# A three-stage kernel whose list scheduler gets other durations, with a smaller DMA scratch, a second row buffer and two more weight slots

## The chip, the cores and the metric

One core of a Trainium2 chip runs the whole program. The metric is the device time of one launch in microseconds (us); lower is better. The core's engines work in parallel and wait for each other by semaphores: PE (TensorE: matmuls; PEld is its weight load), DVE (VectorE), ACT (ScalarE), POOL (GpSimd) and SP (SyncE, which here only issues DMAs, in a fixed order). Each engine works through its own list of instructions in order, so an instruction that waits holds up everything behind it on that engine.

## The reference

Three stages, one feeding the next. B = 4, H = 8, S = 576, D = 64, so 2304 tokens of 512 numbers.

```python
scores = scale * np.matmul(q, k.transpose(0, 1, 3, 2))
ret = scores * Dmat[None, :, :, :]            # decay by distance, causal
x = np.matmul(ret, v)                         # -> 2304 x 512
gate = 1.0 / (1.0 + np.exp(-(x @ w_gate)))    # 512 -> 1536
x = gate * (x @ w_val) @ w_out                # 1536 -> 512
noisy = x @ w_gate2 + np.log1p(np.exp(x @ w_noise)) * noise
top2 = np.argpartition(-noisy, 2, axis=1)[:, :2]     # 2 of 8 experts
out[mask] += w[mask, k, None] * (np.maximum(x[mask] @ w1[e], 0.0) @ w2[e])   # 512 -> 1024 -> 512
```

The weights of the second stage (here called moe1) come as 64-bit floats, all else as 32-bit floats.

## The kernel before, in words

**Arithmetic.** Every large matmul is made as three passes over a value split in two parts (high part and remainder), so each weight and each activation is first split: a cast writes the high part, a subtraction the remainder. 

**Stages.** *Attention* goes by units of two heads: transposes of k and q (PE, L469) that ACT copies out as K (L473), for the later chunk of a sequence a product QF on DVE (L479), scores on PE (L518), the product P of scores and decays on DVE (L525), then av on PE (L535 to L543). *moe1* goes by blocks of 256 tokens and 128-wide slices of the 1536: gv on PE (`up`, L1007), a sigmoid on ACT (L605), sig on DVE (L607), gh on ACT and DVE (L609, L610), then acc on PE (L616). Its first third (half 0, four slices) runs between attention's units, and the partial sums go through a buffer `row` (ACT copy L629 in `part_out`) to DRAM. Half 1 does the other eight slices; `x2_out` (L633 and on) loads the partial sum (L637), adds it (L639), splits the row by 16-bit halves (a copy, in a helper at L283), stores it as x2d (L646), turns it by a DMA transpose on SP (`turn`, L947), joins the halves again (x2T, L283) and makes the routing logits on PE (L668, L671). *Routing* (`route`) takes five groups of token tiles, ranks them (rk, L819), and scatters two table entries per token tile with indirect DMAs of POOL (T, L857). *moe2* loads the tables (L870, L876), gathers an expert's rows on POOL (xr, L913), turns them (xq, L947; for the first two parts xtp on PE, L943), splits them into gxT (L962), then `up` (L1007), hT on ACT and DVE (L1012, L1014), `down` y (L1020), the weighting yo (L1025, L1027) and POOL's scatters of it (L1036). From the second expert on POOL also fetches the rows written before (ag, L1000). Each expert has two parts (s = 0, 1 for the first expert, s = 2, 3 for the second and so on).

**Weights.** `weight64` converts a 64-bit float slice: a DMA r64 (L307), two ACT passes (L308, L310), on DVE the triple L315, L316, L317, an integer add on POOL (L319), a cast on ACT (L320) and a subtraction on DVE (L321). There are 36 such conversions. `weight32` loads raw (L328, three buffers), casts it (L283, on ACT or DVE) and subtracts (L331, on DVE or POOL). Finished weights lie in slots of one ring, "w": NSLOT_A from the start and NSLOT_B more once attention's buffers are given up (`open2`).

**The order.** No engine's list is written by hand. Each operation is declared with an engine (or a choice of engines), a duration from a formula (`t_act`, `t_dve`, `t_fast`, `t_pool`, `t_pe`), a priority, the buffers that it reads and writes, and for a DMA an amount `nbytes` for the shared DMA time line and a `tail` until the data are there. `Order.run` then simulates: at each step it takes, over all engines, the operation that can start first, and among those within .02 us of that on an engine the one of the best priority; LAT is added when an operation waits for another engine. A ring that is full makes the next writer wait. The resulting order is what the engines get. The main lines are:

```python
c.append((s, o.prio, o.seq, o))
t0 = min(x[0] for x in c)
s, p, q, o = min((x for x in c if x[0] <= t0 + .02), key=lambda x: (x[1], x[2]))
dma = max(dma, s + us + 0.6) + o.nbytes
o.end = dma
o.end += o.tail
```

Of the kernel before, what the change touches and what calls it, by code (L numbers as in the profile page):

```python
# [65 lines left out]
P_UNIT, P_CONV, P_MOE1, P_MOE2 = 4.0, 6.0, 1000.0, 2000.0  # L66
P_CONV_OFF2, P_CONV2, LEAD_W, LEAD_A = 80.0, 6.0, 8, 8
P_CONV_OFF, P_X, P_EV, P_ROUTE, P_FILL = 7.0, -700.0, -900.0, -900.0, 900.0
ROWB = 1
DMA_TAIL = 1.0  # L70
P_HALF, TURNED, X2T, X2H, X2P, X2R, XF = 0.0, 14, 1, 1, 2, 1, 1

TURN_FROM = 2
# [11 lines left out]


def t_act(n):
    return .05 + .0009 * n


def t_dve(n):
    return .06 + .00105 * n


def t_fast(n):
    return .06 + .00053 * n


def t_pool(n):
# [20 lines left out]
class Order:  # L120


    LAT = 0.17

    def __init__(self):
        self.ops, self.rings, self.live, self.chain, self.bufs = [], {}, {}, {}, {}
# [138 lines left out]
                    put(d)  # L265


NSLOT_A, NSLOT_B = 18, 6


class Kern:
# [20 lines left out]
    def weight64(self, src, shape, prio):  # L292

        nc, op = self.nc, self.op
        n = 512
        raw = self.buf("r64", lambda _: self.cv.tile([128] + shape[:-1] + [2 * shape[-1]], I32, name="r64", bufs=NCV[0]))
        t1 = self.buf("t1", lambda _: self.cv.tile([128, n], I32, name="t1", bufs=NCV[1]))
        t2 = self.buf("t2", lambda _: self.cv.tile([128, n], I32, name="t2", bufs=NCV[2]))
        w = self.wbuf(shape, "w")
        pat = "p k (f t) -> p (k f) t" if len(shape) == 2 else "p (f t) -> p f t"  # L300

        def word(i):
            return raw.ap.rearrange(pat, t=2)[:, :, i]

        def wv(i):
            return (w.ap.rearrange("p a k f -> p a (k f)") if len(shape) == 2 else w.ap)[:, i]
        op("SP", .5, lambda: nc.sync.dma_start(raw.ap, src), w=[raw], prio=prio - LEAD_W, nbytes=1.45, tail=DMA_TAIL)  # L307
        op("ACT", t_act(n), lambda: nc.scalar.activation(f(t1.ap), f(word(1)), AF.Abs), r=[raw], w=[t1], prio=prio)  # L308

        op("ACT", t_act(n), lambda: nc.scalar.activation(t2.ap, word(0).bitcast(U32), AF.Copy, scale=2.0 ** -29),  # L310
           r=[raw], w=[t2], prio=prio)


        def high():
            nc.vector.tensor_scalar(f(t1.ap), f(t1.ap), E_MIN, E_MAX, op0=ALU.max, op1=ALU.min)  # L315
            nc.vector.tensor_scalar(t1.ap, t1.ap, 3, 0x3fffffff, op0=ALU.logical_shift_left, op1=ALU.bitwise_and)  # L316
            nc.vector.scalar_tensor_tensor(t1.ap, word(1), -0x40000000, t1.ap, op0=ALU.bitwise_and, op1=ALU.bitwise_or)  # L317
        op("DVE", .27 + 2 * t_fast(n) + t_dve(n), high, r=[raw, t1], w=[t1], prio=prio)
        op("POOL", t_pool(n), lambda: nc.gpsimd.tensor_add(t2.ap, t1.ap, t2.ap), r=[t1, t2], w=[t2], prio=prio)  # L319
        op("ACT", t_act(n), lambda: nc.scalar.copy(wv(0), f(t1.ap)), r=[t1], w=[w], prio=prio)  # L320
        op("DVE", t_dve(n), lambda: nc.vector.tensor_sub(wv(1), f(t2.ap), f(wv(0))), r=[t2, w], w=[w], prio=prio)  # L321
        return w

# [309 lines left out]
    def x2_out(self, t, acc, prio):  # L633
        nc, op = self.nc, self.op
        part = self.buf("part", lambda _: self.rt.tile([128, DM], F32, name="part", bufs=X2P))
        row = self.buf("x2", lambda _: self.rt.tile([128, DM], F32, name="x2", bufs=X2R))
        op("SP", .5, lambda: nc.sync.dma_start(part.ap, self.p2d[t * 128:(t + 1) * 128, :]), r=[self.p2[t]], w=[part],  # L637
           prio=prio, nbytes=.73, tail=DMA_TAIL)
        op("DVE", t_dve(DM), lambda: nc.vector.tensor_add(row.ap, acc.ap, part.ap), r=[acc, part], w=[row], prio=prio)  # L639
        self.x2[t] = self.buf(None, None)  # L640

        xh = self.buf("x2h", lambda _: self.rt.tile([128, DM], I32, name="x2h", bufs=X2H))
        op(None, {"ACT": t_act(2 * DM), "DVE": t_fast(2 * DM), "POOL": t_pool(3 * DM)},
           lambda e: self.split(e, xh.ap, row.ap),
           r=[row], w=[xh], prio=prio + P_HALF)
        op("SP", .5, lambda: nc.sync.dma_start(self.x2d[t * 128:(t + 1) * 128, :], xh.ap), r=[xh], w=[self.x2[t]],  # L646
           prio=prio + P_HALF, nbytes=.73, tail=DMA_TAIL)
        xT = self.buf("x2T", lambda _: self.rt.tile([128, KD, 128], F32, name="x2T", bufs=X2T))
        if t < TURNED:
            xq = self.buf("x2q", lambda _: self.rt.tile([128, 2 * KD, 128], U16, name="x2q", bufs=1))  # L650
            op("SP", .5, lambda: self.turn(xq.ap, xh.ap), r=[xh], w=[xq], prio=prio + P_HALF, nbytes=.9, tail=DMA_TAIL)
            for w in range(2):
                op(None, {"ACT": t_act(DM), "DVE": t_fast(DM)}, lambda e, w=w: self.join(e, xT.ap, xq.ap, w), r=[xq], w=[xT], prio=prio + P_HALF)
        else:
            tp = self.buf("x2p", lambda _: self.ps_rt.tile([128, KD, 128], F32, name="x2p", tag="x2p"))

            def transposes():
                for k in range(KD):
                    nc.tensor.transpose(tp.ap[:, k], row.ap[:, k * 128:(k + 1) * 128], self.ident)
            op("PE", .45, transposes, r=[row], w=[tp], prio=prio)  # L660
            op(None, {"ACT": t_act(DM), "DVE": t_dve(DM)}, lambda e: self.copy(e, xT.ap, tp.ap), r=[tp], w=[xT], prio=prio)

        lg = self.buf("lg", lambda _: self.ps_lg.tile([128, 2, 128], F32, name="lg", tag="lg"))
        lT = self.buf("lT", lambda _: self.lT)

        def logits():
            for k in range(KD):
                nc.tensor.matmul(lg.ap[32 * k:32 * k + 32, 0], self.wgn[:, k], xT.ap[:, k], start=True, stop=True)  # L668
        op("PE", .27, logits, r=[xT, self.rset], w=[lg], prio=prio)
        op("ACT", t_act(128), lambda: nc.scalar.copy(lT.ap, lg.ap[:, 0]), r=[lg], w=[lT], prio=prio)  # L670
        op("PE", .11, lambda: nc.tensor.transpose(lg.ap[:, 1], lT.ap, self.ident), r=[lT], w=[lg], prio=prio)  # L671
        self.lgb[t] = self.buf(None, None)
        op("DVE", .25, lambda: nc.vector.tensor_reduce(
            self.lgs[:, t], lg.ap[:, 1].rearrange("p (g e) -> p e g", e=32)[:, :2 * E], axis=mybir.AxisListType.X, op=ALU.add),
            r=[lg], w=[self.lgb[t]], prio=prio)
        for g in GROUPS:
            if t == g[-1]:
                self.route(g, prio)
# [285 lines left out]
    def gather(self, s):  # L964

        op = self.op
# [6 lines left out]
        for t in range(nt):  # L973
# [9 lines left out]
                op("PE", .45, lambda x=x, xf=xf: self.columns(x.ap, xf.ap), r=[xf], w=[x], prio=p)  # L983
            else:
                xq, x = self.buf("xq", self.xq_tile), xf
                op("SP", .5, lambda xq=xq, xr=xr: self.turn(xq.ap, xr.ap), r=[xr], w=[xq], prio=p, nbytes=.9, tail=DMA_TAIL)
                for w in range(2):
                    op(None, {"ACT": t_act(DM), "DVE": t_fast(DM)}, lambda e, xq=xq, xf=xf, w=w: self.join(e, xf.ap, xq.ap, w),
                       r=[xq], w=[xf], prio=p)
# [310 lines left out]
```

## Time and profile before

| | |
|---|---|
| runs | 1124.95 us median of 3 (1123.38 to 1125.94) |
| the profiled execution | 1132.48 us, span 1130.8 us, mean granted TensorE clock 0.982 of full speed |
| busy share of the span | PE 94%, PEld 83%, DVE 52%, ACT 33%, POOL 25% |
| largest groups on PE | gv 339.0 us, up 236.4, y 221.5, acc 178.8 |
| DMA | 120.14 MB, mean 106 GB/s |

A time line row gives the start of a run of like instructions, its length, engine, line, what is written from what, how many, and in brackets how long the engine had stood idle before, and for whom. Rows with "q" (SPq) are DMA issues in the engine's queue; their length is the time that the queue was held, waiting included. A busy share is an average over stages; stages are looked at apart by a table of stretches.

### The profile page before, as it was taken

The numbers are of one execution on the slowest core, as the hardware profiler recorded it, in microseconds if no ns is written. First come the engines' busy times: TensorE is split into PE (matmuls) and PEld (weight loads), VectorE is DVE, ScalarE is ACT, GpSimd is POOL, SyncE is SP. The second block draws the span as 40 slices with busy tenths as digits, with TensorE's granted clock in tenths as the row PEclk, the third lists the DMA queues.
The fourth block names the chain that finished last, engine by engine and source line by source line (L and its number), as shares of the span: only waits on it lengthen the run. The fifth ranks groups of instructions, "written<-read, shape, count | busy, mean of one in ns | idle before, by whom it ended". The sixth has DMA issues, their size and how long they took to land. (4 is left out here: it accounts for less than half of the span.)

```text
span 1130.8 us, 18154 instructions
## 1 busy us (share of the span) xinstructions
PE 1066.9 (94%) x6965; PEld 937.3 (83%) x6966; DVE 591.9 (52%) x1360; ACT 368.5 (33%) x783; POOL 284.5 (25%) x288
## 2 busy tenths in 40 slices
PE   9779997999999999999998898799999999999996
PEld 6546776999889898889988787789888989898985
DVE  4998447322942425332556866546464747474421
ACT  5666325323732322222224323223222323232110
POOL 2322002000310001300205424444434343433230
PEclk9999998999999999999999999899999999999998
DMA  7898316101400511331123427836464756564210
GB/s 183 206 235 204 85 43 173 57 20 38 149 20 1 112 25 33 58 57 25 33 57 122 122 67 183 203 97 187 108 172 123 182 131 187 130 189 92 75 53 14
DMA packets 193564, 120.14 MB, mean 106 GB/s; under 512 B 124286, under 2 KB 169854, under 8 KB 193472
## 3 DMA queue, kind: packets, MB, share of 16 engines
q1 hardware_dynamic: 180480, 94.17, 33.5%
q0 software_dynamic: 12992, 24.75, 7.5%
q8 instruction: 56, 0.92, 0.4%
q14 instruction: 36, 0.29, 0.1%
HBM read 91.23 MB, written 28.94 MB: 106 GB/s over the span
## 5 line engine op out<-in xcount | busy, mean ns | idle before, releaser
L1007 PEld LDWEIGHTS gv<-xs,w 128*128 128x128 f32 x2592 | 329.9, 192 | 15.3 <-DVE sig L607 3.5
L1007 PE MATMUL gv<-xs,w 128*128 128x256 f32 x2592 | 339.0, 285 | 2.9 <-DVE sig L607 2.9
L1007 PE MATMUL up<-gxT,w 128*128 128x256 f32 (+1 forms) x1536 | 236.4, 314 | 9.8 <-DVE hT L1014 9.6
L1007 PEld LDWEIGHTS up<-gxT,w 128*128 128x128 f32 x1536 | 231.4, 192 | 13.8 <-DVE hT L1014 11.6
L1020 PE MATMUL y<-w,hT 128*128 128x512 f32 (+1 forms) x960 | 221.5, 390 | 0.0
L1020 PEld LDWEIGHTS y<-w,hT 128*128 128x128 f32 x960 | 178.0, 188 | 38.1
L616 PE MATMUL acc<-w,gh 128*128 128x512 f32 x648 | 178.8, 406 | 9.1 <-ACT row L629 4.9
L616 PEld LDWEIGHTS acc<-w,gh 128*128 128x128 f32 x648 | 113.7, 192 | 34.4 <-DVE gh L610 5.8
L607 DVE TENSOR_TENSOR sig<-sig,gv 128x256 f32<-128x256 f32 x108 | 45.3, 419 | 170.5 <-ACT sig L605 170.2
L1012 ACT ACTIVATE hT<-up 128x256 fp32r<-128x256 f32 (+1 forms) x128 | 56.2, 439 | 239.2 <-PE up L1007 129.6
L605 ACT ACTIVATE sig<-gv 128x256 f32<-128x256 f32 x108 | 41.5, 384 | 217.8 <-PE gv L1007 213.8
L857 POOL DMA_INDIRECT T<-ent,di x36 | 36.5, 1014 | 272.0 <-DVE ent L853 262.7
L319 POOL TENSOR_TENSOR t<-t,t 128x512 int32<-128x512 int32 x36 | 50.3, 1398 | 188.6 <-ACT t L310 108.1
L1027 DVE SCALAR_TENSOR_TENSOR yo<-y,tab,ag 128x512 f32<-128x512 f32 (+1 forms) x35 | 26.0, 743 | 118.7 <-PE y L1020 118.7
L1014 DVE SCALAR_TENSOR_TENSOR hT<-up,hT 128x256 fp32r<-128x256 f32 (+1 forms) x128 | 62.5, 488 | 47.7 <-ACT hT L1012 47.6
L331 DVE TENSOR_TENSOR w<-raw,w 128x512 fp32r<-128x512 f32 x117 | 79.9, 688 | 7.8 <-ACT w L283 6.6
L913 POOL DMA_INDIRECT xr<-x2d,tab x40 | 42.9, 1073 | 162.2 <-DMA xq<-xr 149.6
L610 DVE TENSOR_TENSOR gh<-sig,gh 128x256 fp32r<-128x256 f32 x108 | 46.3, 428 | 27.3 <-ACT gh L609 27.1
L609 ACT CAST gh<-sig 128x256 fp32r<-128x256 f32 x108 | 43.9, 407 | 46.9 <-DVE sig L607 46.7
L1036 POOL DMA_INDIRECT p2d<-yo,tab x38 | 39.6, 1042 | 56.9 <-DVE yo L1027 44.3
L1036 POOL DMA_INDIRECT out_dram<-yo,tab x35 | 38.4, 1097 | 43.9 <-DVE yo L1027 34.4
L283 ACT CAST w<-raw 128x512 fp32r<-128x512 f32 x53 | 32.7, 619 | 47.2 <-PE y L1020 23.8
(180 smaller groups left out, 947.4 us busy)
## 6 DMA issues: line engine op xcount, KB each, us to landing
raw<-in_moe_w_dram SPq DMA_DIRECT2D x128, 256.0 KB, 3.2
r<-in_moe_w_gate_dram SPq DMA_DIRECT2D x12, 512.0 KB, 4.6
r<-in_moe_w_val_dram SPq DMA_DIRECT2D x12, 512.0 KB, 4.6
r<-in_moe_w_out_dram SPq DMA_DIRECT2D x12, 512.0 KB, 4.4
p2d<-row SPq DMA_DIRECT2D x18, 256.0 KB, 2.0
part<-p2d SPq DMA_DIRECT2D x18, 256.0 KB, 3.7
x2d<-x2h SPq DMA_DIRECT2D x18, 256.0 KB, 3.4
kn<-in_k_dram SPq DMA_DIRECT2D x24, 128.0 KB, 3.7
```

What stands on the lines that cost most here:

```text
L319: op("POOL", t_pool(n), lambda: nc.gpsimd.tensor_add(t2.ap, t1.ap, t2.ap), r=[t1, t2], w=[t2], prio=prio)
L331: lambda e: self.eng(e).tensor_sub(w.ap[:, 1], raw.ap, f(w.ap[:, 0])), r=[raw, w], w=[w], prio=prio)
L607: op("DVE", t_dve(BLK), lambda sig=sig, gv=gv: nc.vector.tensor_mul(sig.ap, sig.ap, gv.ap[:, 1, :]), r=[gv, sig], w=[sig], prio=p)
L609: op("ACT", t_act(BLK), lambda sig=sig, gh=gh: nc.scalar.copy(gh.ap[:, 0, :], sig.ap), r=[sig], w=[gh], prio=p)
L610: op("DVE", t_dve(BLK), lambda sig=sig, gh=gh: nc.vector.tensor_sub(gh.ap[:, 1, :], sig.ap, f(gh.ap[:, 0, :])), r=[sig, gh], w=[gh], prio=p)
L616: nc.tensor.matmul(a[tt].ap, gh.ap[:, p, tt * 128:tt * 128 + 128], wo.ap[:, q, :], start=first and n == 0, stop=last and n == 2)
L913: self.nc.gpsimd.indirect_dma_start(out=xr, out_offset=None, in_=self.x2d[0:n, :], in_offset=bass.IndirectOffsetOnAxis(ap=idx, axis=0), bo ...
L1007: self.nc.tensor.matmul(ps[:, :n], w1[:, p, k, :], xT[:, q, k, :n], start=k == 0 and j == 0, stop=k == KD - 1 and j == 2)
L1012: self.nc.scalar.activation(hT[:, ft, 0, :n], ps[:, :n], AF.Relu)
L1014: self.nc.vector.scalar_tensor_tensor(hT[:, ft, 1, :n], ps[:, :n], 0.0, f(hT[:, ft, 0, :n]), op0=ALU.max, op1=ALU.subtract)
L1020: self.nc.tensor.matmul(y, hT[:, ft, p, t * 128:t * 128 + 128], w2[ft][:, q, c], start=ft == 0 and j == 0, stop=ft == NF2 - 1 and j == 2)
L1036: return self.nc.gpsimd.indirect_dma_start(out=dst[:, :], out_offset=bass.IndirectOffsetOnAxis(ap=idx, axis=0), in_=yo, in_offset=None, bo ...
```

## The change

It alters constants of the planner, the sizes of three resources, and the declared costs of three kinds of DMA:

- `t_act`, `t_dve`, `t_fast` (duration of an ACT or DVE instruction of n elements a partition) and LAT are larger;
- DMA_TAIL goes from 1.0 to 1.4; the r64 load counts 1.6 of DMA time instead of 1.45, with .6 more tail; a turn (both uses of L947) counts 1.25 us on SP instead of .5, less DMA time, and .3 less tail than DMA_TAIL;
- the ring `row` gets a second buffer, the weight slots go from 18 + 6 to 19 + 7;
- the program is built with 4,096 bytes of scratch for POOL's DMAs in place of the default of 16,384.

```diff
-ROWB = 1
-DMA_TAIL = 1.0
+ROWB = 2
+DMA_TAIL = 1.4
...
 def t_act(n):
-    return .05 + .0009 * n
+    return .13 + .0009 * n
 def t_dve(n):
-    return .06 + .00105 * n
+    return .08 + .00112 * n
 def t_fast(n):
-    return .06 + .00053 * n
+    return .1 + .0006 * n
...
-    LAT = 0.17
+    LAT = 0.22
...
-NSLOT_A, NSLOT_B = 18, 6
+NSLOT_A, NSLOT_B = 19, 7
...
-        op("SP", .5, lambda: nc.sync.dma_start(raw.ap, src), w=[raw], prio=prio - LEAD_W, nbytes=1.45, tail=DMA_TAIL)
+        op("SP", .5, lambda: nc.sync.dma_start(raw.ap, src), w=[raw], prio=prio - LEAD_W, nbytes=1.6, tail=DMA_TAIL + .6)
...
-            op("SP", .5, lambda: self.turn(xq.ap, xh.ap), r=[xh], w=[xq], prio=prio + P_HALF, nbytes=.9, tail=DMA_TAIL)
+            op("SP", 1.25, lambda: self.turn(xq.ap, xh.ap), r=[xh], w=[xq], prio=prio + P_HALF, nbytes=.7, tail=DMA_TAIL - .3)
...
-                op("SP", .5, lambda xq=xq, xr=xr: self.turn(xq.ap, xr.ap), r=[xr], w=[xq], prio=p, nbytes=.9, tail=DMA_TAIL)
+                op("SP", 1.25, lambda xq=xq, xr=xr: self.turn(xq.ap, xr.ap), r=[xr], w=[xq], prio=p, nbytes=.7, tail=DMA_TAIL - .3)
...
-    nc = bacc.Bacc("TRN2", target_bir_lowering=False, num_devices=1)
+    nc = bacc.Bacc("TRN2", target_bir_lowering=False, num_devices=1, dynamic_dma_scratch_size=4096)
```

The order moves on every engine. Three places follow; numbers behind names are the program's buffer numbers and differ between the two orders.

First pair: DVE in attention, from the QF product of one unit to the first P product of the next (L315 to L317 and L321 are weight conversions). Before:

```order
L479 TENSOR_TENSOR QF_882<-K_821,gq_113 128x320
L436 TENSOR_TENSOR ks_890<-kn_836,gk_110 128x512
L321 TENSOR_TENSOR w_853<-t2_803,w_853 128x512
L315 TENSOR_SCALAR t1_784<-t1_784 128x512
L316 TENSOR_SCALAR t1_784<-t1_784 128x512
L317 SCALAR_TENSOR_TENSOR t1_784<-r64_704,t1_784 128x512
L315 TENSOR_SCALAR t1_916<-t1_916 128x512
L316 TENSOR_SCALAR t1_916<-t1_916 128x512
L317 SCALAR_TENSOR_TENSOR t1_916<-r64_867,t1_916 128x512
L479 TENSOR_TENSOR QF_953<-K_888,gq_113 128x320
L321 TENSOR_TENSOR w_935<-t2_911,w_935 128x512
L525 TENSOR_TENSOR P_968<-sc_948,gd_112 128x2x320
```

With the change, the same place:

```order
L479 TENSOR_TENSOR QF_866<-K_758,gq_113 128x320
L321 TENSOR_TENSOR w_830<-t2_763,w_830 128x512
L436 TENSOR_TENSOR ks_888<-kn_771,gk_110 128x512
L315 TENSOR_SCALAR t1_786<-t1_786 128x512
L316 TENSOR_SCALAR t1_786<-t1_786 128x512
L317 SCALAR_TENSOR_TENSOR t1_786<-r64_671,t1_786 128x512
L479 TENSOR_TENSOR QF_913<-K_850,gq_113 128x320
L525 TENSOR_TENSOR P_920<-sc_900,gd_112 128x2x320
```

One triple and one L321 fewer stand ahead of the P product.

Second pair: ACT behind attention, up to the row copies L629 and the first L308 whose raw weight is loaded after attention (r64_2027 before, r64_2112 with the change). Before:

```order
L308 ACTIVATE t1_2060<-r64_1285 128x512
L609 CAST gh_2072<-sig_2037 128x256
L320 CAST w_2075<-t1_2022 128x512
L605 ACTIVATE sig_2084<-gv_2029 128x256
L308 ACTIVATE t1_2093<-r64_2027 128x512
L609 CAST gh_2100<-sig_2084 128x256
L310 ACTIVATE t2_2103<-r64_1285 128x512
L629 COPY row_2109<-acc_1753 128x512
```

With the change:

```order
L500 COPY xT3_81<-av_1986 128x320
L320 CAST w_2049<-t1_1341 128x512
L629 COPY row_2057<-acc_1677 128x512
L629 COPY row_2069<-acc_1686 128x512
...
L609 CAST gh_2168<-sig_2139 128x256
L605 ACTIVATE sig_2180<-gv_2127 128x256
L310 ACTIVATE t2_2182<-r64_1449 128x512
L308 ACTIVATE t1_2197<-r64_2112 128x512
L320 CAST w_2210<-t1_2147 128x512
L609 CAST gh_2215<-sig_2180 128x256
```

The row copies now stand ahead of the waiting L308 instead of behind it, side by side.

Third pair: SP at the start of moe2, turns (L947) among the loads of the second expert's weights (L328). Before, raw_7681 is the load whose cast stands ahead of the first hT of s = 2:

```order
L328 DMA raw_7585<-in_moe2_w1_dram 128x4x128
L947 DMA_TRANSPOSE xq_7603<-xr_7562 128x8x128
L328 DMA raw_7612<-in_moe2_w1_dram 128x4x128
L947 DMA_TRANSPOSE xq_7623<-xr_7596 128x8x128
L947 DMA_TRANSPOSE xq_7677<-xr_7634 128x8x128
L328 DMA raw_7681<-in_moe2_w1_dram 128x4x128
```

With the change, where raw_7682 is that load:

```order
L328 DMA raw_7620<-in_moe2_w1_dram 128x4x128
L947 DMA_TRANSPOSE xq_7624<-xr_7575 128x8x128
L947 DMA_TRANSPOSE xq_7639<-xr_7607 128x8x128
L328 DMA raw_7682<-in_moe2_w1_dram 128x4x128
L328 DMA raw_7697<-in_moe2_w1_dram 128x4x128
L328 DMA raw_7700<-in_moe2_w1_dram 128x4x128
L947 DMA_TRANSPOSE xq_7711<-xr_7666 128x8x128
```

Before, seven turns of moe2 stand ahead of that load on SP, now six.

## Rows read from the trace of the kernel before

**Rows 1.** Busy us by stretch: stretch, length, each engine's busy (xinstructions), clock, DMA share, GB/s.
```profile
20.00:110.00 90.00, 73.85 (x663) 51.07 (x660) 85.42 (x165) 61.51 (x136) 27.77 (x19) 0.96 0.87 215
...
172.00:200.00 28.00, 22.21 (x136) 19.93 (x136) 22.08 (x42) 15.66 (x31) 8.84 (x13) 0.88 0.67 178
280.00:320.00 40.00, 36.65 (x246) 33.22 (x245) 35.46 (x55) 26.71 (x52) 12.13 (x9) 0.96 0.35 112
380.00:580.00 200.00, 193.05 (x1401) 175.78 (x1400) 81.59 (x267) 50.07 (x121) 22.50 (x22) 0.99 0.25 48
600.00:660.00 60.00, 52.73 (x358) 45.54 (x357) 43.39 (x114) 26.24 (x53) 24.37 (x21) 0.97 0.50 146
660.00:730.00 70.00, 60.90 (x325) 53.90 (x324) 42.91 (x127) 19.43 (x39) 26.82 (x26) 0.96 0.60 143
740.00:1120.00 380.00, 377.36 (x2116) 341.83 (x2115) 192.40 (x363) 93.79 (x177) 145.59 (x152) 1.00 0.49 129
```

**Rows 2.** Order of time on PE: six of its waits, one from each stretch.
```profile
80.88 0.74 PE L518 MATMUL sc<-K 64*96 64x192 f32 x8 [3.21 <-DVE P L525]
...
187.75 1.65 PE L616 MATMUL acc<-w,gh 128*128 128x512 f32 x3 [4.86 <-ACT row L629]
...
299.66 1.71 PE L1007 MATMUL gv<-xs,w 128*128 128x256 f32 x12 [2.08 <-DVE sig L607]
...
465.02 0.66 PE L668 MATMUL lg<-x2T,wgn 128*32 128x128 f32 x8 [2.33 <-DVE x2T L283]
...
615.20 1.06 PE L943 MATMUL xtp<-ident,xf 128*128 128x128 f32 x4 [2.17 <-issue]
...
725.09 7.08 PE L1007 MATMUL up<-gxT,w 128*128 128x384 f32 x23 [5.73 <-DVE hT L1014]
```

**Rows 3.** Groups by form, DVE's four steps of a conversion: busy us, mean ns, idle before.
```profile
L321 DVE TENSOR_TENSOR w<-t,w 128x512 fp32r<-128x512 f32 x36 | 29.0, 816 | 2.9 <-POOL t L319 2.0 <-ACT w L320 0.9
L317 DVE SCALAR_TENSOR_TENSOR t<-r,t 128x512 int32<-128x512 int32 x36 | 28.9, 802 | 1.2
...
L315 DVE TENSOR_SCALAR t<-t 128x512 f32<-128x512 f32 x36 | 22.8, 634 | 3.4 <-ACT t L308 3.3
...
L316 DVE TENSOR_SCALAR t<-t 128x512 int32<-128x512 int32 x36 | 21.2, 588 | 1.2
```

**Rows 4.** Order of time on ACT and on SP's queue, behind attention.
```profile
185.70 0.66 ACT L308 ACTIVATE t<-r 128x512 f32<-128x512 f32 x1 [6.11 <-DMA r<-in_moe_w_out_dram]
...
181.66 0.38 SPq L307 DMA_DIRECT2D r<-in_moe_w_out_dram  x1
```

**Rows 5.** Order of time on PE, at full clock and without waits.
```profile
211.70 3.76 PE L1007 MATMUL gv<-xs,w 128*128 128x256 f32 x30
215.29 1.55 PE L616 MATMUL acc<-w,gh 128*128 128x512 f32 x6
```

**Rows 6.** Order of time on SP's queue and on DVE, at the start of moe2.
```profile
708.95 1.23 SPq L947 DMA_TRANSPOSE xq<-xr  x1
...
711.00 7.14 SPq L947 DMA_TRANSPOSE xq<-xr  x2
718.26 1.88 SPq L328 DMA_DIRECT2D raw<-in_moe_w_dram  x3
...
723.41 0.43 DVE L283 CAST w<-raw 128x512 fp32r<-128x512 f32 x1 [5.04 <-DMA raw<-in_moe_w_dram]
```

**Rows 7.** Order of time on DVE, one L316.
```profile
75.91 1.38 DVE L316 TENSOR_SCALAR t<-t 128x512 int32<-128x512 int32 x1
```

**Rows 8.** DMA issues by line: count, median us to landing.
```profile
xr<-x2d,tab POOLq DMA_INDIRECT x40, 3.5
p2d<-yo,tab POOLq DMA_INDIRECT x38, 3.0
...
ag<-p2d,tab POOLq DMA_INDIRECT x35, 3.3
out_dram<-yo,tab POOLq DMA_INDIRECT x35, 3.6
```

## The prediction, made before the changed kernel ran

> **What bounds the kernel now.** The first view is the table of busy time by stretch of the program [rows 1]: the reader is to set PE's busy time against each stretch's length, and DVE's beside it. PE is busy nearly throughout, no other engine is, except DVE in the first stretch; so the order can win only where PE stands still or runs slowly. In the last 380 us PE idles 2.6 us. The idle time lies ahead of it: 16.2 us (90.00 less 73.85) while attention, the first part of moe1 and the conversion of its weights run together; 5.8 us just behind attention; 3.4 us in the second burst of conversions; 7.0 us in the stretch with the logits; 7.3 and 9.1 us where the routing and the start of moe2 lie. That is 48.8 us. The same six stretches are those below a granted clock of 1.00; (1 - clock) times length gives 3.6 + 3.4 + 1.6 + 2.0 + 1.8 + 2.8 = 15.2 us more.
>
> The order of time on PE then names who ended each long wait [rows 2]: the P product of DVE (3.21 us), a row copy of ACT (4.86), sig of DVE (2.08), the copy x2T (2.33), an xtp after which nothing is named (2.17), hT of DVE (5.73). None of these operations is long; each is late because something else stood in front of it on its engine. Which order the engines get is what the change alters.
>
> **The change, part by part.** No operation of the computation is added or removed. The planner's constants, one more row buffer, two more weight slots and a smaller scratch move work and take waits away. The sum is made against the profiled execution, 1132.48 us, which is 7.53 us above the median of the runs shown (1124.95); at the end I scale by 1124.95/1132.48 = 0.9934.
>
> *Attention (20 to 110).* DVE is busy 85.42 of these 90 us, PE 73.85 [rows 1]: DVE is the bound here. A conversion costs DVE .634 + .588 + .802 + .816 = 2.84 us by its four rows [rows 3], and a P product that PE waits for stands behind them: ahead of the one PE waited for at 80.88 [rows 2] come two triples and two L321. With the new costs fewer stand there (first pair of fences: one triple instead of two between the two QF). Counted over the whole order, L315 and L321 ahead of the k-th P product go from 10 and 8 to 8 and 6 (k = 32), 14 and 13 to 11 and 10 (k = 52), 19 and 17 to 15 and 14 (k = 64); from k = 76 it is 21 and 18 against 22 and 19. With each instruction at the mean of its form, DVE's work ahead of a product less PE's work ahead of the matmul that takes it is at most 16.8 us before, which agrees with the 16.2 us of idle PE, and at most 10.0 after. The term is that difference, rounded down, **-6**. Bounds: -2 (the waits move to K and QF, of which ACT and DVE have their own queues) and -10 (three to four conversions by 2.84).
>
> *Behind attention (172 to 200).* PE's wait of 4.86 at 187.75 ends with ACT's row copy [rows 2]; ACT stood 6.11 us before L308, up to 185.70, for a raw weight whose DMA SP issued only at 181.66, behind the loads of moe2 and the four T fills [rows 4]. The row copy stood behind that L308. In the new order (second pair) both row copies come first, which the second row buffer allows, and the L308 that waits for the first late weight (r64_2112) stands 13 places later. SP still issues it behind three fills, so it lands about as late, some 13 us after the end of attention at 172 (13.7 before, up to 185.70). Until PE wants the gh that is queued behind it, it has 78 gv and 18 acc matmuls: 78 x .120 + 18 x .23 = 13.5 us, from a run of 30 gv in 3.59 us and one of 6 acc [rows 5]. With L308, L320, L609 and L610 behind the landing, none over the .634 us of L315 by much [rows 3] and 2.2 together, gh is ready after some 15.2, so 1.7 us stay, and I allow 1 for the next weight. From 5.8: **-3**, bounds 0 and -5.8. Next late is gh_2215.
>
> *Second burst (280 to 320).* At most two triples now stand ahead of a sig, where three stood; sig ended 2.08 us of waiting [rows 2] of 3.4 in all. **-2**, bounds 0 and -3.4.
>
> *Logits (380 to 580).* Six waits like that of 465.02 [rows 2]; PE meets a logit matmul before its x2T has come back from the turn. The work that PE does, at the same durations, between the last acc matmul of a token tile and its L668 rises from 7.13 to 7.82 us for the first tile of a pair and from 10.6-11.0 to 13.1 for the second: a turn is now planned with 1.25 us on SP and a longer tail. Waits of 1 to 2.3 us shrink by .7 to 2.3. **-4** of 7.0, bounds -1 and -6.9.
>
> *Routing (600 to 660).* The first xtp stands at least 18 gv matmuls further on, so the 2.17 us at 615.20 [rows 2] should go; of the 7.3 us the rest is as likely to grow as to shrink. **-2**, bounds +2 and -5.
>
> *Start of moe2 (660 to 730).* The 5.73 us at 725.09 [rows 2] go back through one chain: hT stood on DVE behind a cast, which waited 5.04 us for a raw weight, issued at 718.26, behind the seventh turn, in which SP's queue stood 7.14 us [rows 6]. In the new order (third pair) that weight's DMA (raw_7682) stands behind six turns, before the one that waited: it can go at about 712.5, when the sixth turn, begun at 711.00, is issued (the fifth took SP 1.23 us), some 6 us earlier. PE has 41.7 us of work from the last rank to this stage against 42.7, so it arrives no later. Some 3 us of wait for xr and the turn may remain ahead of gxT. Both xtp's now stand behind all y matmuls. **-5** of 9.1, bounds 0 and -9.
>
> *The rest (740 to 1119).* PE idles 2.6 us of 380 [rows 1]; casts stand a little nearer to hT, but two more slots let them start earlier. **0**, bounds +3 and -2.6. POOL takes 19 of the L331 subtractions where it took 11; it is busy 145.59 of these 380 us and DVE 192.40 [rows 1], so both have room. The price on DVE is in the row of 75.91, where L316 takes 1.38 us while POOL adds [rows 7], against .588 on its mean [rows 3]: .8 us for each of the 8, 6.4 in all, beside 188 free: **0**. By the Trainium skill, "SBUF — State Buffer", section "Who interferes with whom", a DVE instruction with two SBUF inputs or in a two-port mode and one of GpSimd that reads SBUF exclude each other; the row of 75.91 agrees, and the rule speaks against handing POOL more: by it the term would be up to +6.4 if every one of the 8 met a DVE instruction that PE waits for.
>
> *Clock.* The six stretches lost 15.2 us to it, and a low clock follows PE's long waits: the stretch with the largest share idle (21%) has the lowest, 0.88 [rows 1]. About half of the idle time goes, but short waits stay in all stretches. **-2**, bounds 0 and -8.
>
> Sum: -6 - 3 - 2 - 4 - 2 - 5 - 2 = **-24**, so 1108.5 us for a profiled execution and 1108.5 x 0.9934 = **1101** for the median.
>
> **The rivals.**
> 1. *The waits move on.* PE comes earlier to the next wait, and what ends that keeps its length: in attention DVE must still do 22 and 19 conversions by k = 76; the gathers and turns of moe2 wait for each other and not for PE (SP's 7.14 [rows 6]). Then half the sum arrives: -12, 1120.5 profiled, **1113**. For it: DVE's 85.42 of 90. Against it: 16.8 and 16.2 agree.
> 2. *No change.* The costs are only a plan; waits of DMAs decide, and they vary. 1123 to 1127. Against it: three waits (4.86, 2.17, 5.73) have their place changed, not their odds.
> 3. *Slower: the scratch.* With 4,096 bytes of scratch for the indirect DMAs, POOL might have to wait for the last one to land before it writes the next. There are 148 of them, nearly all from 660 on, which land in 3.0 to 3.6 us each [rows 8], against an issue of about .96 us (145.59 us in 152 instructions of POOL [rows 1]). One at a time they would take 40 x 3.5 + 38 x 3.0 + 35 x 3.3 + 35 x 3.6 = 496 us. POOL's other work from 660 on is about 172 - 148 x .96 = 30 us (172 are its 26.82 and 145.59 [rows 1]), so 526 us would have to fit into the 460 that are there: 1101 + 66 = **1167**. It decides from (460 - 30)/148 = 2.9 us for each, so one in flight is slower, and two (1.7 each) are not. Nothing in the profile shows how many the old scratch held. By the Trainium skill, "DMA: Bandwidth & Descriptors", sections "SWDGE vs HWDGE vs iDMA" and "The descriptor swizzle", GpSimd writes 16-byte descriptors to rings in SBUF and a large 128-partition transfer has 9 on each side for each of 16 engines; an estimate, with a ring of 4,096 bytes for each engine and side, from that page is 4096/16/9 = 28 transfers in the scratch, far from one, and no run here shows it. By that rule this rival costs nothing.
>
> **How the numbers follow.** Forecast .62, rival 1 .20 (of it .02 beyond no change), rival 2 .08, rival 3 .06, and .04 for a slower order in the last 380 us, where 2.6 us of idle time leave more to lose than to win. A measurement of this kernel tells 0.2% (2.2 us) from no change. Faster: .62 + .18 = .80; same .08; slower .12 (.02 + .06 + .04). Range: at the low end the terms lie half way to their best bounds (-10, -5.8, -3.4, -6.9, -5, -9, -2.6, -8, in all -50.7): -37.4, 1095.1 x 0.9934 = 1088. At the upper end it takes in rival 1 and stops short of no change: 1121. I take 1087 to 1121; slower and no change lie outside.
>
> **What would show it.** In the profile after: idle PE in the attention stretch near 10 us and no wait of 3 us for a P product; no wait for a row copy behind attention; waits for x2T below 1 us; no hT wait of 5 us at the start of s = 2; the mean clock above its old value. Wrong it is if PE's idle time falls by less than 12 us, if the waits come back under other names, or if POOL's indirect DMAs stand more than .3 us apart after one another and are released by a DMA.

## The result, and the profile after

The changed kernel takes 1094.61 us (median of 4, 1092.92 to 1096.74) beside 1125.45 us (1123.38 to 1128.43) for the kernel before in the same measurement: a ratio of 0.9728, 95% interval 0.9708 to 0.9749, or 30.8 us less. Forecast were 1101 us and a range of 1087 to 1121. In later measurements the kernel before itself took about 1136 us in three and 1126.64 in a fourth, with one chip in both groups, so what follows compares ratios, and two variants within one measurement where they are close.

The profiled execution after took 1092.92 us, span 1091.2, 1.7 below its median; that of before was 7.5 above its own. The profiles therefore differ by 39.6 us of span, 9 more than the medians do, and the terms below are read against 39.6.

The table by stretch, after, with the stretches moved to the same places of the program and in the order of [rows 1]:

```profile
20.00:110.00 90.00, 81.62 (x740) 56.56 (x737) 85.27 (x172) 64.37 (x144) 27.20 (x19) 1.00 0.88 216
168.00:196.00 28.00, 25.05 (x176) 22.46 (x172) 23.01 (x44) 18.55 (x37) 9.08 (x13) 1.00 0.73 211
278.00:318.00 40.00, 37.33 (x255) 33.56 (x254) 28.53 (x45) 19.86 (x41) 9.48 (x7) 1.00 0.25 80
360.00:560.00 200.00, 198.95 (x1465) 181.04 (x1464) 85.83 (x276) 53.00 (x128) 22.73 (x22) 1.00 0.24 50
575.00:632.00 57.00, 51.45 (x358) 45.66 (x358) 45.35 (x116) 25.32 (x54) 26.21 (x24) 0.97 0.53 149
632.00:702.00 70.00, 63.18 (x331) 55.73 (x331) 44.84 (x126) 18.23 (x36) 28.92 (x28) 0.95 0.60 142
702.00:1084.00 382.00, 382.00 (x2155) 346.94 (x2154) 193.44 (x355) 97.78 (x186) 159.14 (x165) 1.00 0.48 130
```

Idle PE falls from 16.2 to 8.4 us in attention, from 5.8 to 3.0 behind it, from 3.4 to 2.7 in the second burst, from 7.0 to 1.0 in the logits, from 7.3 to 5.6 in the routing, from 9.1 to 6.8 at the start of moe2 and from 2.6 to 0 in the rest. The clock column is 1.00 in five of the seven stretches, where [rows 1] has it in one.

The order of time on PE, after; the waits that answer to [rows 2]:

```profile
80.91 0.44 PE L469 MATMUL tr<-ident,kn 128*128 128x128 f32 x2 [1.50 <-ACT K L473]
...
183.05 0.73 PE L616 MATMUL acc<-w,gh 128*128 128x512 f32 x2 [1.09 <-ACT gh L609]
...
303.03 1.20 PE L616 MATMUL acc<-w,gh 128*128 128x512 f32 x4 [1.17 <-DVE gh L610]
...
443.99 0.43 PE L668 MATMUL lg<-x2T,wgn 128*32 128x128 f32 x8 [0.90 <-ACT x2T L283]
...
598.19 0.86 PE L943 MATMUL xtp<-ident,xf 128*128 128x128 f32 x4 [3.18 <-DVE sp L776]
...
694.67 17.01 PE L1007 MATMUL up<-gxT,w 128*128 128x384 f32 x84 [3.75 <-DVE hT L1014]
```

These are the longest waits of their stretches. Four are small now. Two are not: one of 3.18 us that before did not have, and the hT wait at the first slices of s = 2, 3.75 where it was 5.73.

### The profile page after: what moved, and what is told of

Same layout as the page of the kernel before. It is cut to its first block, busy times and chain, and to the rows that moved or that the text cites. A ratio compares the mean times of both kernels' runs of the same rounds, so it can differ in the third digit from the quotient of the medians.

```text
span 1091.2 us, 18157 instructions
## 1 busy us (share of the span) xinstructions
PE 1055.6 (97%) x6965; PEld 928.0 (85%) x6966; DVE 592.9 (54%) x1349; ACT 367.9 (34%) x786; POOL 295.4 (27%) x296
## 4 chain that ended last, share of the span: by engine, by line
PE 57%; issue 25%; DMA 7%; DVE 7%; POOL 2%; ACT 1%; SPq 0%; POOLq 0%; ACTq 0%; DVEq 0%
PE up L1007 19%; PE y L1020 18%; PE gv L1007 9%; PE acc L616 5%; POOL T L857 2%; PE sc L518 2%; DMA xr<-x2d,tab 1%; DMA xq<-xr 1%; PE av L543 1%; PE dec L390 1%; DMA r<-in_moe_w_out_dram 1%; PE tr L469 1%; DVE P L525 1%; DMA T<-ent,di 1%; DVE t L316 1%
## 5 line engine op out<-in xcount | busy, mean ns | idle before, releaser
L1007 PE MATMUL gv<-xs,w 128*128 128x256 f32 x2592 | 333.8, 284 | 1.5 <-DVE sig L607 1.5
L1007 PEld LDWEIGHTS gv<-xs,w 128*128 128x128 f32 x2592 | 324.5, 191 | 11.9 <-DVE sig L607 1.9
L1007 PE MATMUL up<-gxT,w 128*128 128x256 f32 (+1 forms) x1536 | 234.0, 312 | 5.7 <-DVE hT L1014 4.7
L616 PE MATMUL acc<-w,gh 128*128 128x512 f32 x648 | 175.3, 401 | 4.8 <-DVE gh L610 3.6
L331 DVE TENSOR_TENSOR w<-raw,w 128x512 fp32r<-128x512 f32 x109 | 76.1, 704 | 5.0 <-ACT w L283 3.0
L610 DVE TENSOR_TENSOR gh<-sig,gh 128x256 fp32r<-128x256 f32 x108 | 52.5, 487 | 24.2 <-ACT gh L609 24.1
L283 ACT CAST w<-raw 128x512 fp32r<-128x512 f32 x61 | 37.7, 619 | 36.9 <-PE y L1020 19.9
```

The costliest lines, as they stand in the source:

```text
L331: lambda e: self.eng(e).tensor_sub(w.ap[:, 1], raw.ap, f(w.ap[:, 0])), r=[raw, w], w=[w], prio=prio)
L610: op("DVE", t_dve(BLK), lambda sig=sig, gh=gh: nc.vector.tensor_sub(gh.ap[:, 1, :], sig.ap, f(gh.ap[:, 0, :])), r=[sig, gh], w=[gh], prio=p)
L616: nc.tensor.matmul(a[tt].ap, gh.ap[:, p, tt * 128:tt * 128 + 128], wo.ap[:, q, :], start=first and n == 0, stop=last and n == 2)
L1007: self.nc.tensor.matmul(ps[:, :n], w1[:, p, k, :], xT[:, q, k, :n], start=k == 0 and j == 0, stop=k == KD - 1 and j == 2)
```

## The experiments

**The parts by themselves.**

```diff
e1:  +dynamic_dma_scratch_size=4096                        (nothing else)
e2:  all planner costs; NSLOT 18, 6; ROWB 1; default scratch
e3:  NSLOT 19, 7; ROWB 2; scratch 4096; old planner costs
e4:  t_act, t_dve, t_fast, LAT only
e5:  DMA_TAIL, r64, turn costs only
```

> The kernel before with the scratch of 4,096 bytes and nothing else: every engine has the order of before. My theory (the order made the gain, the scratch only makes room): ratio 1.000, within 0.2%. Rival (POOL waits for earlier indirect DMAs to land): over 1.01, and gaps between POOL's back-to-back indirect DMAs grow from 0.3 us. Its profile is also a second look at the order of before: the span of before's profile was 7.5 us above the median, and if that was the draw, idle PE here is about 55 us with a mean clock above 0.982.

> All planner costs of the change, but 18 + 6 slots, one row buffer and the old scratch. Theory (costs set the order, buffers add a little): ratio 0.974 to 0.980, that is 24 to 30 of the 31 us; the attention order ahead of the P products is that of the change, so idle PE from 20 to 110 is 8 to 10 us, and waits for x2T fall below 1 us; what is missing is behind attention, where the second row copy stands 6 places behind the first. Rival (the slots and the row buffer carry the gain): ratio 0.99 or more.

> Scratch, second row buffer and two more slots with the old costs. The order is nearly that of before: conversions ahead of the P products and matmuls between logits are unchanged, and the row copies still stand behind the ACT instruction that waits for the late weight. Theory: ratio 0.995 to 1.000; the wait for the row copy of 4 to 5 us is still there. Rival (buffers carry the gain): 0.985 or less.

> Only the durations of ACT and DVE instructions and LAT are those of the change; DMA costs and buffers are those of before. Ahead of the 52nd P product stand 11 begun and 10 finished conversions as in the change (14 and 13 before), and the first three pairs of logits are as far apart as in the change. If engine times make the gain by the attention order: idle PE from 20 to 110 near 9 us and ratio 0.980 to 0.986. If the DMA costs (the r64 load, the turn) make it: ratio above 0.992.

> Only the DMA costs of the change (DMA_TAIL, the r64 load, the turns); durations of ACT and DVE, LAT and all buffers are those of before. Ahead of the 52nd P product stand 13 begun and 11 finished conversions (14 and 13 before, 11 and 10 with the change); the logits of a pair are 17.8 and 20.6 us apart as with the change. If the engine times carry the gain: ratio 0.990 to 0.997, with 12 to 14 us idle from 20 to 110. If the later turn carries it through the logits: ratio below 0.988 and no wait for x2T over 1 us, with the old idle time in attention.

| to the kernel before | ratio | 95% interval | idle PE, 20 to 110 |
|---|---|---|---|
| e1 scratch only | 0.9948 | 0.9931 to 0.9965 | 15.7 |
| e2 all costs | 0.9831 | 0.9799 to 0.9864 | 9.0 |
| e3 buffers and scratch | 0.9989 | 0.9967 to 1.0011 | 15.2 |
| e4 engine times | 0.9853 | 0.9819 to 0.9887 | 10.7 |
| e5 DMA costs | 0.9888 | 0.9867 to 0.9908 | 12.4 |

The last column is 90 less PE's busy time in the first row of each one's table by stretch; of e2, e4 and e5 in turn:

```profile
20.00:110.00 90.00, 81.04 (x716) 56.73 (x715) 83.62 (x168) 63.15 (x141) 23.48 (x18) 0.98 0.86 210
```
```profile
20.00:110.00 90.00, 79.31 (x679) 54.05 (x679) 79.31 (x163) 60.06 (x136) 23.96 (x17) 0.94 0.89 206
```
```profile
20.00:110.00 90.00, 77.64 (x696) 54.33 (x692) 86.68 (x170) 62.56 (x139) 27.16 (x19) 0.98 0.88 218
```

The costs carry most of the gain, and they overlap: engine times alone give 1.5%, DMA costs alone 1.1%, both 1.7%. Idle PE in attention follows the number of conversions that the order has begun ahead of the 52nd P product: 14 in e1, 13 in e5, 11 in e4 and e2 (15.7, 12.4, 10.7, 9.0 us). Either set of costs moves it, but not by the same waits. From 20 to 110 PE waits 5.9 us for P products in e1, 5.7 in e5 and not once in e4; for K, which ACT copies, it waits 6.6, 4.3 and 7.6 us. The largest entry of each (total, times, longest), of e5 and of e4:

```profile
PE sc L518 <- DVE P L525: 4.9, 3, 2.3
```
```profile
PE sc L518 <- ACT K L473: 4.5, 3, 2.4
```

So the attention term's mechanism, a P product that is late behind conversions, is seen to go with the engine times; with the DMA costs alone it is K and QF that PE waits for less. e2's and e5's ratios missed what was expected of them, e2's by .003 above and e5's by .001 below; e3's and e4's came as expected.

The logits differ between the two sets. The longest wait for x2T in e5, which has the new cost of a turn, and in e4, which has the old one:

```profile
461.61 0.65 PE L668 MATMUL lg<-x2T,wgn 128*32 128x128 f32 x8 [2.29 <-ACT x2T L283]
```
```profile
456.29 0.66 PE L668 MATMUL lg<-x2T,wgn 128*32 128x128 f32 x8 [0.98 <-ACT x2T L283]
```

e5 has three such waits over 1 us, e4 none. Neither spaces these logits as the change does: PE's work between the last acc matmul of a pair's first tile and its L668 is 6.8 us before, 6.8 in e4 and in e5 (the tiles whose logits start at 415.47 and 420.27) and 7.5 only with the change (407.44). In e4 x2T is ready sooner, 7.5 us after the start of L639 for that tile where before has 8.3 and e5 8.4. Why it is ready sooner is open.

e1 is a surprise, 0.5% faster in the order of before, where 0.2% at most was expected; it is taken up below. e3 then holds a loss: with the scratch's half per cent in it, its ratio is 0.9989. By the old costs the extra slot lets one more conversion stand ahead of the last P products (22 begun and 19 finished from k = 72, where before has 21 and 18). Attention's last copy on ACT comes 3.7 us later than in e1, the two rows being e1's and e3's:

```profile
172.80 0.43 ACT L500 COPY xT<-av 128x320 f32<-128x320 f32 x1 [2.68 <-PE av L543]
```
```profile
176.53 0.43 ACT L500 COPY xT<-av 128x320 f32<-128x320 f32 x1 [2.68 <-PE av L543]
```

e3 changes the row buffer and the other slots as well, so that the slot is the cause is worked out from the order, not shown by itself.

**The change, less one resource.**

```diff
a1:  the change
a2:  -NSLOT_A, NSLOT_B = 19, 7     +18, 6
a3:  -ROWB = 2                     +1
a4:  -dynamic_dma_scratch_size=4096  +2048
```

> The changed kernel once more, beside the three variants of it that follow, so that they share a chip. Theory: ratio 0.971 to 0.975 as in the first measurement. If the part that costs alone did not give (0.9831 against 0.9728) lay in the chip of that measurement and not in the buffers, the ratio here is nearer to 0.979.

> The change with 18 + 6 weight slots instead of 19 + 7; costs, row buffer and scratch stay. Theory (the slots let the second expert's weights be loaded and cast earlier): the routing and the start of moe2 lose 3 to 5 us, ratio to the kernel before 0.975 to 0.979. Rival (slots idle, PE never waits for a slot): within 0.2% of the changed kernel.

> The change with one row buffer instead of two; the rest stays. The second row copy behind attention now stands 8 places behind the first on ACT, behind two weights' steps. Theory: it costs what PE waits there for gh or for the row, 0 to 2 us: 0.000 to 0.002 over the changed kernel's ratio. Rival (the row buffer alone removed the 4.9 us): 0.004 or more over it, with a wait for a row copy of over 3 us at about 185.

> The change with a scratch of 2,048 bytes instead of 4,096, no other edit. After the last matmul the span goes on for 11.3 us in every profile with the default scratch of 16,384 bytes and for 6.0 to 6.4 us in every one with 4,096. If this tail grows with the scratch by (11.3 - 6.3)/12288 us per byte, it is 5.5 us here, and the ratio lies 0.001 below the changed kernel's. If there is no such law, the tail stays 6.0 to 6.4. If POOL already waits for its own transfers at this size, gaps between its back-to-back indirect DMAs exceed 0.3 us and the kernel is slower.

Measured to the kernel before: a1 0.9769 (0.9746 to 0.9793), a2 0.9767 (0.9739 to 0.9795), a3 0.9787 (0.9761 to 0.9812), a4 0.9790 (0.9764 to 0.9817). a1's ratio is that of the costs times that of the scratch, 0.9831 x 0.9948 = 0.978: costs and scratch are enough to explain it. The 0.971 to 0.975 expected of a1, taken over from the first measurement, missed; why that measurement came out lower is not shown. The slots give nothing that can be told (a2 against a1): the rival held, my theory fell. a4's tail is 5.8 us where 5.5 was expected, and its time is not told from a1's. a3 is .002 over a1, as the theory had it, and their intervals overlap; but its trace has the wait for a row copy that the rival named, on ACT and then on PE:

```profile
180.57 0.59 ACT L629 COPY row<-acc 128x512 f32<-128x512 f32 x1 [4.44 <-DMA p2d<-row]
```
```profile
181.21 0.97 PE L616 MATMUL acc<-w,gh 128*128 128x512 f32 x3 [3.19 <-ACT row L629]
```

With one buffer the second copy waits 4.44 us until the first row has gone out, and PE 3.19 us. That both parts are needed here does not follow. e2 has the new costs, one buffer and the old slots; its second copy waits too, but PE has enough other work and waits for no row copy. The copy in e2, and e2's stretch behind attention, in which PE idles 2.2 us:

```profile
178.23 0.59 ACT L629 COPY row<-acc 128x512 f32<-128x512 f32 x1 [2.25 <-DMA p2d<-row]
```
```profile
170.00:198.00 28.00, 25.84 (x175) 22.86 (x174) 24.66 (x45) 16.73 (x35) 9.40 (x12) 1.00 0.71 202
```

e4, also with one buffer, idles 1.3 us there; e1, in the order of before, 5.3, and e3, with two buffers and the old costs, keeps a wait for the row copy of 4.67 us. So the new engine times take the wait away, and the second buffer shows an effect only in the order with the larger slots, a3's.

**The tail.**

```diff
b1, the kernel before:  +dynamic_dma_scratch_size=8192
```

> The kernel before with a scratch of 8,192 bytes and no other edit; the order is that of before. The time from the end of the last matmul to the end of the span was 11.3 us with the default of 16,384 bytes in four profiles, 6.0 to 6.4 with 4,096 and 5.8 with 2,048. If the tail is linear in the scratch between 4,096 and 16,384, it is 7.7 to 8.1 us here and the ratio 0.996 to 0.998. If it is a step (some threshold above 4,096), it is 11.3 or about 6.2, and the ratio 1.000 or 0.995.

Each program ends with the same scatter on POOL. Span, and that last row, of before, b1, e1 and a4, with scratches of 16,384, 8,192, 4,096 and 2,048 bytes:

```profile
span 1130.8 us, 18154 instructions
...
1120.32 0.97 POOL L1036 DMA_INDIRECT out_dram<-yo,tab  x1 [4.50 <-DVE yo L1027]
```
```profile
span 1123.8 us, 18154 instructions
...
1117.47 0.97 POOL L1036 DMA_INDIRECT out_dram<-yo,tab  x1 [4.50 <-DVE yo L1027]
```
```profile
span 1129.7 us, 18154 instructions
...
1124.11 0.97 POOL L1036 DMA_INDIRECT out_dram<-yo,tab  x1 [4.50 <-DVE yo L1027]
```
```profile
span 1108.7 us, 18157 instructions
...
1103.74 0.97 POOL L1036 DMA_INDIRECT out_dram<-yo,tab  x1 [4.19 <-DVE yo L1027]
```

From the start of that scatter to the end of the span it is 10.5, 6.3, 5.6 and 5.0 us. (The expectations count from the last matmul, .8 us earlier: 11.3, 7.1, 6.4 and 5.8.) The tail is far longer at 16,384 bytes, whatever the order of the work: e2 and e4 with the new orders and the old scratch have 10.5 too. Below that the steps are not clear of the spread, since the programs with 4,096 bytes have 5.0 to 6.1 (f2 and a3).

What fills it are two rows of POOL's queue behind the last scatter (shortest, median, longest in ns), of before and of e1:

```profile
L1099 POOLq INC_SWDGE_SEM  x1: 1737/1737/1737, 1121.8 to 1121.8; - x1
L1296 POOLq DRAIN  x3: 40/107/6435, 1123.5 to 1130.5; - x3
```
```profile
L1099 POOLq INC_SWDGE_SEM  x1: 512/512/512, 1125.6 to 1125.6; - x1
L1296 POOLq DRAIN  x3: 40/107/2790, 1126.1 to 1129.4; - x3
```

The first is 1.2 us shorter and the longest DRAIN 3.6, together the 4.9 us between the two tails. In b1 they take .92 and 3.09 us, in a4 .37 and 2.04. The first shrinks at each step; the DRAIN has 2.0 to 3.3 us in the programs with 4,096.

The tail is not linear: b1 came out under the 7.7 to 8.1 expected, its ratio, 0.9981 (0.9963 to 0.9999), inside what was expected. Of e1's 0.52% (5.9 us of 1135.79) 4.9 us are this tail.

**The new wait, and a better kernel.** Around the wait of 3.18 us at 598.19, the changed kernel on DVE (the two L610 of that stretch: shortest, median, longest in ns) and on POOL:

```profile
L610 DVE TENSOR_TENSOR gh<-sig,gh x2: 419/2512/4605, 592.7 to 593.1; 128x256 fp32r<-128x256 f32 x2
```
```profile
593.64 3.74 POOL L331 TENSOR_TENSOR w<-raw,w 128x512 fp32r<-128x512 f32 x3
```

```diff
f2, on the change (weight32):
-        op(None, {"DVE": t_dve(512), "POOL": t_pool(512)},
+        op(None, {"DVE": t_dve(512)},
g1, on f2 (gather):
-            ..., w=[xr], prio=p, nbytes=.73, tail=DMA_TAIL)
+            ..., w=[xr], prio=p, nbytes=.73, tail=DMA_TAIL + 1.5)
```

> The change, with all weight subtractions of L331 on DVE and none on POOL (19 in the changed kernel). In the changed kernel's trace three of them run in a row on POOL (593.64 to 597.38), and on DVE two L610, .42 us each elsewhere, take 4.94 us over the same time; PE then waits 3.18 us for DVE at the second xtp. Theory (POOL's subtraction locks out a DVE instruction with two inputs in SBUF): no DVE instruction of that form over 1 us at that place, the mean of L610 back from 475-487 to 421-428 ns, that wait of PE gone, and 2 to 4 us less than the changed kernel, ratio to the kernel before about 0.974 where the change has 0.977. Rival (DVE is short of time there and the work it takes back costs as much): ratio 0.976 to 0.980.

> The kernel with the subtractions on DVE, and beside that the gather xr planned 1.5 us longer, near the 3.5 us and more that it takes to land. SP then plans the turns later and puts weight loads ahead of them. In the changed kernel's first profile SP's queue stood 8.97 us in two turns at 680 and PE waited 3.75 us for hT at the first slice of s = 2. If that wait comes from loads behind turns that wait for a gather: it falls below 1.5 us, and the ratio lies 0.001 to 0.003 below that of the kernel with the subtractions on DVE. If the gathers are needed that early for PE: PE waits for gxT instead and the ratio is the same or higher.

f2 has 0.9756 (0.9733 to 0.9779), g1 0.9711 (0.9689 to 0.9733), in one measurement. In f2 no L610 is long any more, at that place or elsewhere (the longest takes 427 ns), its second xtp waits 1.01 us, and the mean of L610 goes back from 487 ns to 420. The four at that place:

```profile
L610 DVE TENSOR_TENSOR gh<-sig,gh x4: 416/418/419, 612.0 to 621.4; 128x256 fp32r<-128x256 f32 x4
```

The mechanism is shown; the time is not, since f2's interval covers a1's ratio and a wait of 3.17 us for hT stands at the start of s = 2. g1 plans the gather's landing longer; there the two hT waits are short:

```profile
707.12 4.45 PE L1007 MATMUL up<-gxT,w 128*128 128x384 f32 x24 [1.11 <-DVE hT L1014]
712.87 7.41 PE L1007 MATMUL up<-gxT,w 128*128 128x384 f32 x41 [1.30 <-DVE hT L1014]
```

Each is under the 1.5 us expected, together 2.4. g1 is faster than f2, beside which it was measured: none of its six times is over 1105.91 us, none of f2's five under 1106.98. It gained .0045, more than the .001 to .003 expected. That it is faster than the change is not shown: its interval lies wholly below a1's (0.9746 to 0.9793), measured apart from it, but holds the 0.9728 of the change's first measurement.

## Why the prediction was right, point by point

- **Attention (-6).** Right: idle PE 16.2 to 8.4, 7.8 less, and no P product is waited for longer than .8 us in this stretch. The waits for DVE's P and QF, which the sum is about, go from 8.1 to 1.7 us, 6.4 less; those for K, ACT's copy, from 7.7 to 4.9, which the count of DVE's conversions did not cover. That the sum over the order gave 16.8, close to all 16.2 us of idle time, is in part luck, since nearly half of these are waits for K. In e4, e5 and e2 idle time falls in step with the conversions ahead, in e5 by the waits for K and QF.
- **Behind attention (-3).** Right in size: 5.8 to 3.0. The row copy is waited for no more; what stayed is 1.09 for gh and smaller ones, where 1.7 and 1 were allowed. The part given to the second buffer, "which the second row buffer allows", was not needed for PE's wait to go: e2 and e4 lose it with one.
- **Second burst (-2).** Too large: 3.4 to 2.7. The sig waits went, gh waits (L610) came. This was rival 1 in one stretch.
- **Logits (-4).** The size was near in the first pair of profiles, 5.9 (7.0 to 1.0), and the wait for x2T is .90 where 2.33 stood. PE's work ahead of a first logit rose by .7 us as counted (6.8 to 7.5). The reason given for it was too narrow: "a turn is now planned with 1.25 us on SP and a longer tail" alone (e5) leaves the work at 6.8 and waits of 1.5 to 2.3 us. The gain did not come back in a1: the waits for x2T stay away there (.3 us), but PE idles 8.4 us, half of it before matmuls for which the trace names no wait (last section).
- **Routing (-2).** 1.7 measured, but not as told: the 2.17 at the first xtp went, and the 3.18 at the second came. The step that failed is the pricing of eight more subtractions on POOL "at .8 us for each of the 8, beside 188 free: 0". Three in a row held one L610 on DVE for 4.6 us; over the whole run the L610 group grew from 428 to 487 ns a piece, 108 x .059 = 6.4 us, 4.2 of them in this one instruction. The Trainium skill ("SBUF — State Buffer", "Who interferes with whom") has the rule, an exclusive lock between a DVE instruction with two SBUF inputs and GpSimd's reads, and the prediction put the term "up to +6.4" by it: the trace agrees with the rule (the L610 ends at 597.7, .3 us after the last of the three on POOL), and f2, without POOL's subtractions, has none. The wait at the second xtp comes back in a1 to a4, 3.18 to 3.21 us each time. What was missed is where these three stand: in a stretch in which DVE is busy 45 of 57 us and PE soon waits for it, so that the room in the 380 us behind it is of no use.
- **Start of moe2 (-5).** Half in this profile: 9.1 to 6.8. The hT wait is 3.75 and not the 0 to 3 allowed for gxT. The late load was to go "at about 712.5, some 6 us earlier", and no cast waits for a weight there any more. What came instead is the turn itself: SP's queue stands in two turns, ACT and DVE wait for the rows of the first, and DVE then works without a pause up to the hT that PE waits for. Of the changed kernel, SP's queue, DVE's two rows, and how long the turns and then the gathers took to land (shortest, median, longest):

```profile
679.97 8.97 SPq L947 DMA_TRANSPOSE xq<-xr  x2
```
```profile
687.88 0.47 DVE L283 COPY xf<-xq 128x512 uint16<-128x512 uint16 x1 [5.95 <-DMA xq<-xr]
...
694.06 0.55 DVE L1014 SCALAR_TENSOR_TENSOR hT<-up,hT 128x384 fp32r<-128x384 f32 x1
```
```profile
DMA to landing us min/median/max: 3.0/3.4/7.8
```
```profile
DMA to landing us min/median/max: 3.3/3.9/7.9
```

  The first of the two turns is the one of 7.8 us, and the gather for which the second waited the one of 7.9. In a1, the same order, SP stands 5.08 us in these two turns and PE's waits for hT are short:

```profile
712.68 4.46 PE L1007 MATMUL up<-gxT,w 128*128 128x384 f32 x24 [0.66 <-DVE hT L1014]
718.04 7.96 PE L1007 MATMUL up<-gxT,w 128*128 128x384 f32 x48 [0.90 <-DVE hT L1014]
```

  So the 3.75 us hang on two slow transfers of one execution, and the forecast for this order was nearer than that profile says. In f2 DVE does wait for a weight again (3.76 us, up to 713.23) ahead of PE's 3.17; g1 moved loads ahead of turns by planning the gather longer, and its waits are 1.11 and 1.30, shorter than f2's and no shorter than a1's.
- **The rest (0).** 2.6 us of idle time went to 0, the best bound.
- **Clock (-2).** Mis-sized in this pair of profiles: the stretches lost 15.2 us to it before and .03 x 57 + .05 x 70 = 5.2 after, 10 less, and PE's busy time for the same matmuls falls by 11.3. In e1 and a1, two profiles from measurements in which the kernel before took about 1136 us, it falls by 2.5 (1067.3 to 1064.8). PE's busy time of before and after:

```profile
PE 1066.9 (94%) x6965; PEld 937.3 (83%) x6966; DVE 591.9 (52%) x1360; ACT 368.5 (33%) x783; POOL 284.5 (25%) x288
```
```profile
PE 1055.6 (97%) x6965; PEld 928.0 (85%) x6966; DVE 592.9 (54%) x1349; ACT 367.9 (34%) x786; POOL 295.4 (27%) x296
```

  In the first profile after, the granted clock stays at 1.00 through attention, where it was 0.96, and it falls where the 3.18 and 3.75 us stand. In a1 it is 0.98 in attention, although no wait there is over 1.3 us, so the length of the longest wait does not settle it.
- **The tail: no term.** 10.5 to 5.6 us, 4.9 less. The prediction looked at the scratch only as something POOL might wait for.

The sum by these readings is -7.8 - 2.8 - .7 - 5.9 - 1.7 - 2.3 - 2.6 - 10 - 4.9 = -38.7 of the profiles' -39.6. Against the medians' 30.8 the forecast of 24 was short by the tail and by part of the clock; two terms were given back in part, as rival 1 said, and not half of the whole. Beside a1 the gain is 25.9 us; less the scratch's part (0.9769 / 0.9948 = 0.982) some 20 us are left for what the prediction had terms for. That the repeat's 25.9 is so near to 24 is therefore in part luck: the tail, which had no term, makes up for terms that came out smaller. **Rival 3** (POOL waits for its transfers) did not come: in the changed kernel and in a4, with a quarter and an eighth of the scratch, POOL's back-to-back issues stay .30 us apart, and e1 is faster, not slower. One gather in each (745.78 in the changed kernel) starts after some 6 us that end on nothing the trace names; PE waits for nothing there. The same gather in e2, which has the old scratch, comes after 5.80 us that end on a turn, so most of this wait is not the small scratch's. The prediction's estimate of 28 transfers, worked out from the Trainium skill ("DMA: Bandwidth & Descriptors", sections "SWDGE vs HWDGE vs iDMA" and "The descriptor swizzle"), spoke against this rival, and the runs agree with it so far: how many transfers a scratch holds was not measured.

## What to carry to other kernels

A planned order is worth as much as its durations: with ones nearer to the trace for the engines alone (a cast of 128x512 on DVE takes .43 us [rows 6]; .33 was planned, now .41), the same program gained 1.5%. About 9 of its 16 us are told apart: 5.0 in attention and 4.0 behind it, where shorter queues of conversions stand in front of operations that PE waits for. After such a change look first for what the planner cannot see: two engines that hold each other up, a queue that stands behind one waiting transfer, a gather that lands later than planned. And price a resource that is made smaller from both sides; here the smaller scratch cost nothing that the runs show and shortened the end of the program.

## What the runs showed of the hardware that was not expected

- The time from the last indirect DMA to the end of the program depends on the scratch reserved for such DMAs: 10.5 us at 16,384 bytes, 6.3 at 8,192, 5.0 to 6.1 at 4,096 and 5.0 at 2,048. POOL's queue spends it in an INC_SWDGE_SEM (1.74 us at 16,384, .92, .50 and .37 at the smaller ones) and a DRAIN (6.44 against 2.0 to 3.3). What they wait for no trace shows.
- One DVE subtraction of two SBUF tiles, .42 us by itself, took 4.6 us beside three POOL subtractions in a row, and ended .3 us after the last of them.
- In every profile from the measurements in which the kernel before took 1136 us, PE lost time in the logits to waits that end on nothing the profile names; before, after and b1 have none there. In a1 (PE idle 8.4 us from 360 to 560, 4.5 of them such waits; 1.0 in the first profile of the same program):

```profile
446.71 0.28 PE L1007 MATMUL gv<-xs,w 128*128 128x256 f32 x1 [0.31 <-issue]
447.44 0.28 PE L1007 MATMUL gv<-xs,w 128*128 128x256 f32 x1 [0.45 <-issue]
448.15 0.28 PE L1007 MATMUL gv<-xs,w 128*128 128x256 f32 x1 [0.42 <-issue]
```

  What holds them is open.
